# Retention and a GELU layer on one core: turned rows 8 bytes apart, v on SyncE's queue, and a shorter warm-up

## The chip, the cores and the metric

The kernel runs on one core of a Trainium2 chip. The core has TensorE (PE) for matrix products, VectorE (DVE), ScalarE (ACT) and GpSimd (POOL) for elementwise work, and SyncE (SP), which here only starts transfers. Transfers can be started from the queues of SP, ACT and POOL. The metric is device time in microseconds (us), the median of several runs.

## The reference

Eight batches of eight heads; 576 tokens, 64 values a head. Each score is weighted with a decay that depends on the distance of the two tokens, and nothing after the query counts. The heads of a token, side by side, are the 512 inputs of a two-layer network with exact GELU.

```python
scores = scale * np.matmul(q, k.transpose(0, 1, 3, 2))
gamma = 1.0 - 2.0 ** (-5.0 - np.arange(H, dtype=np.float32))
rel = pos[:, None] - pos[None, :]
Dmat = np.where(rel >= 0, gamma[:, None, None] ** rel[None, :, :], 0.0)
ret = np.matmul(scores * Dmat[None], v)
x = np.ascontiguousarray(ret.transpose(0, 2, 1, 3)).reshape(B * S, H * D)   # 4608 x 512
h = x @ w_in                                                                # 512 x 2048
out = (0.5 * h * (1.0 + erf(h / sqrt(2)))) @ w_out                          # 2048 x 512
```

All inputs and the output are fp32; the kernel computes in bf16 with fp32 sums.

## The kernel before

**Chunks and units.** A sequence of 576 tokens is cut into four chunks of 128 and a tail of 64. A unit is one chunk of one batch, 128 tokens with all eight heads; the tails of two batches make one unit. There are 36 units and nine blocks of four units (512 tokens) for the network. Groups (up to two units, the same chunk of the two batches of a pair) go through the retention together: 22 groups, of which the first four are single first chunks.

**Retention of a group.** Within a chunk the decay is split: a key's part is multiplied into v (`scaled_v`, giving `vh`, with the factors `dv`), a query's part is multiplied into the result (`evacuate`, factors `dqT`), and a mask of zeros and ones stands between (`masked`, factors `msk`). Earlier chunks come in as a state u = sum of k v, kept by `state` and applied by `cross`. For a first chunk (`raw`: units 0 to 3, 18, 19, 27, 28) there is no state; its mask `near` holds the whole decay, its v goes into `inner` unscaled, and its result is only cast, by DVE or ACT, whichever the planner finds earlier free (`either`).

**Turning q and k.** Scores need q and k with the head values on the partitions. Up to group 7, PE turns them (`turn`) and DVE or ACT copies the result. From group 8 on (`BY_DVE`) they are loaded in another shape: partition p of a 32-row block holds tokens 4p to 4p+3 (tails: 2p and 2p+1), and `turn_dve` transposes blocks of 32 by 32 elements of 4 bytes, each a pair of bf16 values, on DVE. The turned rows of one token then stand side by side with those of the other tokens of its partition, so that neighbours in DVE's writing order are 16 bytes apart (8 in a tail). `scores` and `cross` read them with `cols, y`: every second bf16 value, 128 columns in a row. `state` needs k unturned too, so from unit 11 on (groups of two units) k is loaded a second time (`kn`).

**Loads.** POOL's queue starts the loads, which convert to bf16 on the way, in the order of the list `ORDER` and then group by group as `reload` adds them: q, k, second k, v. At most eight are on their way: each issue waits for the one eight earlier. Only unit 0's q and k come as fp32, over the queues of SP and ACT, and are cast. SP's queue starts the output stores. POOL also scales v for units 26 and up.

**The network.** Each block is two layers of products, `hT` then `oT`; most are done with seven half-size products in place of eight (`mlp2_fast` with accumulators `fa`, `fb`; for the last three blocks `mlp1_fast` with `ha`, `hb`), for which DVE forms sums of operands (`g_sum`, line 675, and others). They start as soon as four units have their x.

**Who sets the order.** Nothing is decided on the chip. While the program is built, a planner keeps an estimated clock for each engine (`T`, advanced by `on` and `pe`), picks the retention step or product that it estimates to be ready, and writes the instructions of every engine in that order. An engine then works strictly in its order and waits for semaphores. Before the first data come, PE runs products of zeros (`warm`, and eight at line 1050). Constants such as `dv`, `dqT` and a first small Gelu that loads ACT's table (`warm_act`) wait in the list `later` until the planner's clock has reached their time.

Of the kernel before, what the change touches and what calls it, by code (L numbers as in the profile page):

```python
# [9 lines left out]
FP32 = mybir.dt.float32  # L10
# [7 lines left out]
def kernel(  # L18
# [46 lines left out]
    raw = [i for i in range(N_U) if units[i][1] == 0]  # L65
# [4 lines left out]
    N_LD = 5  # L70
    N_QKT = 3
    N_KN = 4
    VH_POOL = 26
# [8 lines left out]
    FPOOL = 0.55  # L82
# [28 lines left out]
    zeros = const.tile([128, 512], BF16, name="zeros")  # L111
# [10 lines left out]
    nc.scalar.activation(step, lgT, AF.Exp, scale=float(C))  # L122
    val = const.tile([128, 1, 128], FP32, name="val")
    pos = const.tile([128, 1, NCI], FP32, name="pos")
    far = const.tile([128, 1, 128], FP32, name="far")
    ident = const.tile([128, 1, 128], BF16, name="ident")
    near = const.tile([128, 2, HP, 128], FP32, name="near")
    msk = const.tile([128, 1, 128], FP32, name="msk")
    msk2 = const.tile([128, 1, TAIL], FP32, name="msk2")
# [3 lines left out]
    dqT = const.tile([128, HP, S - C], FP32, name="dqT")  # L133
# [36 lines left out]

    def make_dq(hp):
        nc.scalar.activation(dqT[:, hp, 0:C], val[:, 0, :], AF.Exp, scale=lgT[:, hp], bias=off[:, hp])
# [3 lines left out]
    later += [(9.0, "act", 0.41, lambda hp=hp: make_dq(hp)) for hp in range(HP)]  # L176
    later += [(9.0, "act", 1.45, lambda: nc.scalar.activation(warm_act, ln_scale, AF.Gelu))]
# [32 lines left out]
    def tiles_of(i):  # L210
        g = groups[group_of[i]]
        if i not in loaded:
# [3 lines left out]
            else:  # L216
# [9 lines left out]
                loaded[i] = (qk, ld_pool.tile([128, H, D], BF16, tag="v", bufs=9, name="v_ld"), kn)  # L226
        return loaded[i]

    def load(what, i):
# [8 lines left out]
        if what == "dq":  # L238
            assert i - 1 in dq_done
            dq_done.add(i)  # L240
            finish_later()
            n = min(C, S - i * C)
            nc.gpsimd.tensor_tensor(dqT[:, :, (i - 1) * C:(i - 1) * C + n], dqT[:, :, (i - 2) * C:(i - 2) * C + n],
                                    step.to_broadcast([128, HP, n]), op=ALU.mult)
            on("pool", 1.2)
            return
# [19 lines left out]
        src = {"q": q, "k": k, "n": k, "v": v}[what]  # L266
        for jj in (j,) if j is not None else range(2):
            n = C if j is not None else TAIL
            if what == "n":
                dst = kn[:, :, jj]  # L270
            elif what == "v":
# [4 lines left out]
            land[what, i] = sw_dma(0.9, 0.9) if j is not None else sw_dma(0.68, 0.5)  # L276

    tiles_of(0)
    land["q", 0], land["k", 0] = 4.5, 4.6
    cast_due = {("q", 0): (loaded[0][0][:, 0], first["q32"]), ("k", 0): (loaded[0][0][:, 1], first["k32"])}  # L280
    ORDER = ("wi0 io k1 q1 v0 v1 wi1 q2 k2 v2 wi2 k3 q3 v3 wi3 wi4 wi5 wi6 wi7 wo0 wo1 wo2 wo3 wo4 wo5 wo6 wo7 "
# [894 lines left out]
```

## Time and profile before

| | |
|---|---|
| median of 3 runs (lowest, highest) | 300.25 us (299.87, 300.6) |
| the profiled execution, and its span | 299.83 us, 298.1 us |
| granted TensorE clock, mean | 0.996 |
| busy in the span: PE, DVE, ACT, POOL | 285.2 us, 231.2 us, 135.9 us, 158.2 us |
| PE products and weight loads in the profile | 3693 and 3720 |
| bytes read and written by transfers | 42.47 MB, 9.44 MB |

The page cuts the span into 40 equal slices of 7.45 us and gives each engine a digit, its busy share in tenths. A group of instructions is one line of the kernel with one operation: number, busy time in us, mean duration in ns, then the idle time of the engine ahead of them and what ended it. A row of the waits names who waited, for whom, the total in us, how often and the longest. A row of the timeline gives start, length, engine, line, operation, output and inputs. Products overlap: a product's record goes on past the start of the next.

### The profile page before, as it was taken

To read this page: it belongs to the slowest core of one execution; us is meant where nothing else is said; L and a number is where in the kernel's file an instruction comes from. 1 tells how busy PE (TensorE), PEld (TensorE's weight loads), DVE (VectorE), ACT (ScalarE), POOL (GpSimd) and SP (SyncE) were. 2 spreads that over 40 slices of the span, in tenths; PEclk is the share of its full clock that TensorE was granted. 3 is DMA by queue.
4 is the path that set the end of the run, shared out by engine and by line. 5 is a ranking of instruction groups with operands and counts; after the bars stand their busy time and mean duration, and the time that the engine had idled before them with its cause. 6 is when DMAs were issued, how large, how long until landed. Compare 5 with 4: busy or idle time off the path is not lost.

```text
span 298.1 us, 8709 instructions
## 1 busy us (share of the span) xinstructions
PE 285.2 (96%) x3693; PEld 211.5 (71%) x3720; DVE 231.2 (78%) x430; ACT 135.9 (46%) x262; POOL 158.2 (53%) x231
## 2 busy tenths in 40 slices
PE   7999999998999999999999999999999999999994
PEld 2578656887756656766666656567888888888883
DVE  3872039999999999996770699847997999898851
ACT  5546315844254354343445433534453555546421
POOL 8976798899999988989889941000000000000000
PEclk9999999999999999999999999999999999999998
DMA  9999999999999999999999610201001201201114
GB/s 141 168 186 204 182 170 189 166 135 131 121 162 135 138 141 150 110 160 120 192 151 132 78 38 2 73 2 37 35 2 70 74 0 73 71 2 62 45 55 124
DMA packets 111415, 31.50 MB, mean 106 GB/s; under 512 B 89105, under 2 KB 107025, under 8 KB 111377
## 3 DMA queue, kind: packets, MB, share of 16 engines
q0 software_dynamic: 103744, 20.99, 83.8%
q1 hardware_dynamic: 6592, 9.70, 9.6%
q8 instruction: 29, 0.48, 0.6%
q10 hardware_dynamic: 1040, 0.26, 0.4%
q14 instruction: 10, 0.07, 0.1%
HBM read 42.47 MB, written 9.44 MB: 174 GB/s over the span
## 4 chain that ended last, share of the span: by engine, by line
PE 46%; POOL 24%; DMA 13%; DVE 9%; issue 5%; ACT 1%; DVEq 0%; POOLq 0%; ACTq 0%
PE fa L707 13%; POOL qkb_ld L261 11%; PE fb L707 10%; PE hT L603 7%; PE ha L812 7%; DMA qk_ld<-in_q_dram 6%; PE hb L812 5%; POOL v_ld L275 5%; DMA qkb_ld<-in_q_dram 3%; DMA w_out<-in_moe_w_out_dram 3%; POOL early L275 3%; DVE ret L452 2%; POOL w_in L234 2%; DVE qkT L380 2%; DVE s L675 1%
## 5 line engine op out<-in xcount | busy, mean ns | idle before, releaser
L603 PE MATMUL hT<-x,w_in 128*128 128x512 bf16 (+2 forms) x522 | 92.2, 314 | 2.0 <-DVE x L333 0.5
L603 PEld LDWEIGHTS <-w_in 128*128 128x128 bf16 x544 | 49.4, 98 | 24.5 <-issue 0.9
L707 PEld LDWEIGHTS <-g_all 128*128 128x128 bf16 x512 | 49.5, 98 | 11.6 <-issue 0.7
L608 ACT ACTIVATE g_all<-hT 128x512 bf16<-128x512 f32 x64 | 38.1, 597 | 42.6 <-PE hT L603 40.0
L707 PEld LDWEIGHTS <-s 128*128 128x128 bf16 x384 | 37.0, 98 | 8.3 <-issue 0.3
L693 DVE TENSOR_TENSOR o_sb<-fb,t 128x256 f32<-128x256 f32 x48 | 19.9, 416 | 22.3 <-ACT t L335 11.7
L817 ACT ACTIVATE g_all<-tt 128x512 bf16<-128x512 f32 x36 | 22.6, 630 | 30.2 <-DVE tt L825 30.1
L261 POOL DMA_DIRECT2D qkb_ld<-in_k_dram x56 | 31.1, 594 | 5.6 <-DMA v_ld<-in_v_dram 2.6
L707 PE MATMUL fa<-w_out,g_all 128*128 128x256 bf16 x256 | 33.1, 273 | 0.1
L452 DVE TENSOR_TENSOR ret<-sc,msk 128x512 bf16<-128x512 f32 x48 | 29.6, 671 | 2.8 <-PE sc L425 1.7
L261 POOL DMA_DIRECT2D qkb_ld<-in_q_dram x56 | 31.1, 593 | 0.3 <-issue 0.3
L275 POOL DMA_DIRECT2D v_ld<-in_v_dram x36 | 30.4, 862 | 1.4 <-DMA w_out<-in_moe_w_out_dram 0.8
L825 DVE TENSOR_TENSOR tt<-hb,tt 128x512 f32<-128x512 f32 x36 | 24.5, 687 | 5.2 <-ACT tt L335 2.8
L611 ACT ACTIVATE g_all<-hT 128x512 bf16<-128x512 f32 (+1 forms) x36 | 19.4, 549 | 14.4 <-PE hT L603 14.2
L380 DVE STREAM_TRANSPOSE qkT<-qkb_ld 128x512 f32<-128x512 f32 (+1 forms) x28 | 25.0, 945 | 0.0
L335 ACT COPY t<-fa 128x256 f32<-128x256 f32 x35 | 13.0, 371 | 21.1 <-PE fa L707 21.1
L275 POOL DMA_DIRECT2D kn_ld<-in_k_dram x22 | 19.8, 907 | 2.0 <-DMA qkb_ld<-in_q_dram 1.1
L812 PEld LDWEIGHTS <-ws 128*128 128x128 bf16 x192 | 18.8, 98 | 2.2
L583 DVE TENSOR_TENSOR x<-o_ps,dqT 128x512 bf16<-128x512 f32 (+1 forms) x32 | 18.2, 608 | 1.2 <-PE o_ps L560 1.2
L333 DVE COPY qkT<-qk_ps 128x512 bf16<-128x512 bf16 x10 | 3.9, 419 | 17.4 <-PE qk_ps L368 17.4
L707 PE MATMUL fa<-wt,g_all 128*128 128x256 bf16 x128 | 16.5, 273 | 0.2 <-ACT t L335 0.2
L707 PE MATMUL fb<-w_out,s 128*128 128x256 bf16 x128 | 16.4, 273 | 0.2
(112 smaller groups left out, 455.3 us busy)
## 6 DMA issues: line engine op xcount, KB each, us to landing
out_dram<-o_sb SPq DMA_DIRECT2D x31, 256.0 KB, 2.7
v_ld<-in_v_dram POOLq DMA_DIRECT2D x28, 128.0 KB, 4.7
qkb_ld<-in_q_dram POOLq DMA_DIRECT2D x44, 64.0 KB, 4.2
qkb_ld<-in_k_dram POOLq DMA_DIRECT2D x44, 64.0 KB, 3.7
kn_ld<-in_k_dram POOLq DMA_DIRECT2D x22, 128.0 KB, 4.3
w_in<-in_moe_w_in_dram POOLq DMA_DIRECT2D x8, 256.0 KB, 6.9
w_out<-in_moe_w_out_dram POOLq DMA_DIRECT2D x8, 256.0 KB, 10.0
out_dram<-o_sb SPq DMA_DIRECT2D x8, 128.0 KB, 3.0
```

The lines of the kernel that those rows point to most:

```text
L261: nc.gpsimd.dma_start(qk[p0:p0 + 32, "qk".index(what), 0:HP * per].rearrange("p (h x) -> p h x", h=HP), {"q": q, "k": k}[what][2 * bp + jj ...
L275: nc.gpsimd.dma_start(dst, src[2 * bp + jj, :, ci * C:ci * C + n, :].rearrange("h s d -> s h d"))
L380: nc.vector.transpose(dst, src)
L452: nc.vector.tensor_tensor(r, t, by, op=ALU.mult)
L603: nc.tensor.matmul(hT[:, m - m0, :], lhsT=w_in[:, cc, m * 128:m * 128 + 128], rhs=x_tiles[t][:, cc, lo:hi], start=(cc == 0), stop=(cc == N ...
L608: nc.scalar.activation(g_all[:, t % 2, :, m0, :], hT.rearrange("p n (a c) -> p (n a) c", a=2), AF.Gelu)
L611: nc.scalar.activation(g_of(t, 2 * lo // TOK)[:, m0:m0 + n, lo_:lo_ + hi - lo], hT, AF.Gelu)
L693: nc.vector.tensor_tensor(dst, src, f[key], op=ALU.add)
L707: nc.tensor.matmul(dst, lhsT=x[:, kk, :], rhs=y[:, kk, :], start=(name in "125" and kk == 0), stop=(kk == HK - 1), skip_group_check=True)
L812: nc.tensor.matmul(dst[:, m, :], lhsT=a[:, cc, c0:c0 + 128], rhs=y[:, cc, :], start=(name in "125" and m == 0 and cc == 0), stop=(cc == HC ...
L817: nc.scalar.activation(g_of(t, part)[:, m0:m0 + 2], src, AF.Gelu)
L825: nc.vector.tensor_tensor(f[key], f["b"][1], f[key], op=ALU.add)
```

## The change

- The turned rows of a long group are written in two halves of two tokens a partition each, so that neighbours are 8 bytes apart. For queries the halves are tokens 4p, 4p+1 and 4p+2, 4p+3, and `turned_q` reads them back in the natural order; for keys the halves are the even and the odd tokens, and `turned_k` reads them one after the other.
- Everything that stands with a key follows its order: the second k (`kn`) and v are loaded as two transfers of 64 rows, even tokens to partitions 0 to 63 and odd ones to 64 to 127; there is a mask `mskp` and there are factors `dvp` for that order (`make_skewed`, six small DVE operations and one on ACT).
- v of units 11 to 35 comes over SP's queue as fp32 (`load_v`, tiles `v32`, four buffers), asked for up to four units ahead of the scores; `scaled_v` reads it.
- First chunks 18, 19, 27, 28 are treated like the others: scaled v, mask, and `evacuate` with factors `dqT` for chunk 0, which POOL makes from chunk 1's by the factor `back`.
- POOL scales v from unit 20 on instead of 26. Load buffers for q and k: 4 instead of 5; buffers of turned tiles: 4 instead of 3. Some tiles share buffers (`zeros`, `far` with v32; `near` with q and k; the first turned tiles with `kn`).
- Six warm-up products instead of eight, other planner estimates, and unit 0's v is loaded ahead of unit 1's q and k.
- `put` may send the second half of a last store over ACT's queue.

```diff
-    raw = [i for i in range(N_U) if units[i][1] == 0]
+    raw = [i for i in range(N_U) if units[i][1] == 0 and group_of[i] not in BY_DVE]
-    N_LD = 5
-    N_QKT = 3
+    N_LD = 4
+    N_QKT = 4
-    VH_POOL = 26
+    VH_POOL = 20
-    FPOOL = 0.55
+    FPOOL = 0.6
+    N_V32 = 4
+    N_WARM = 6
+    V_LEAD = 4
...
+    def make_skewed():
+        p = pos[:, :, 0:1]
+        nc.vector.tensor_scalar(skew, p, 64.0, -127.0, op0=ALU.is_ge, op1=ALU.mult)
+        nc.vector.tensor_tensor(skew, skew, p, op=ALU.add)
+        nc.vector.tensor_tensor(mskp, val, skew.to_broadcast([128, 1, 128]), op=ALU.subtract)
+        nc.vector.tensor_scalar(mskp, mskp, 0.0, None, op0=ALU.is_ge)
+        nc.vector.tensor_tensor(posp, pos, skew.to_broadcast([128, 1, NCI]), op=ALU.add)
+        nc.vector.tensor_tensor(dvp, lgh.to_broadcast([128, H, NCI]), posp.to_broadcast([128, H, NCI]), op=ALU.mult)
...
+    later += [(8.5, "dve", 0.8, make_skewed), (9.0, "act", 0.3, lambda: nc.scalar.activation(dvp, dvp, AF.Exp, scale=-1.0, bias=ln_scale))]
...
+    def load_v(i):
+        bp, ci, j = units[i]
+        v32[i] = ld_pool.tile([128, H, D], FP32, tag="v32", bufs=N_V32, name="v32")
+        for e in range(2):
+            src = v[2 * bp + j, :, ci * C + e:ci * C + C:2, :] if j is not None else v[2 * bp + e, :, ci * C:ci * C + TAIL, :]
+            nc.sync.dma_start(v32[i][64 * e:64 * e + 64], src.rearrange("h s d -> s h d"))
...
+        if what == "n":
+            for e in range(2):
+                nc.gpsimd.dma_start(kn[64 * e:64 * e + 64, :, j], k[2 * bp + j, :, ci * C + e:ci * C + C:2, :].rearrange("h s d -> s h d"))
+                land[what, i] = sw_dma(0.68, 0.45)
+            return
...
-    ORDER = ("wi0 io k1 q1 v0 v1 wi1 q2 k2 v2 wi2 k3 q3 v3 wi3 ...
-             ... q11 k11 q12 k12 n11 n12 v11 v12").split()
+    ORDER = ("wi0 io v0 k1 q1 v1 wi1 q2 k2 v2 wi2 k3 q3 v3 wi3 ...
+             ... q11 k11 q12 k12 n11 n12 dq0").split()
...
+    def turned(n, x):
+        us = 1 if units[groups[n][0]][2] is None else 2
+        t = qkT_of(n)[:, x].rearrange("p h s -> p (h s)")[:, 0:HP * us * 128]
+        return us, t.rearrange("p (h u b t y) -> p h u b t y", h=HP, u=us, t=2, y=2)
...
-        dst = qkT[:, x, :, 0:rows, :].rearrange("p h s y -> p h (s y)").bitcast(FP32).rearrange("p h (b t) -> p h t b", b=32)
+        dst = qkT_of(n)[:, x].rearrange("p h s -> p (h s)")[:, 0:2 * m].bitcast(FP32)
+        if us == 1 or x == 0:
+            src, dst = src.rearrange("p h (u t) e -> p (h u) t e", u=us), dst.rearrange("p (h b t) -> p h t b", t=2, b=32)
+        else:
+            src, dst = src.rearrange("p h (t u) e -> p h t u e", u=us), dst.rearrange("p (h u b t) -> p h t u b", h=HP, t=2, b=32)
         nc.vector.transpose(dst, src)
...
+    def turned_q(n, sl, hp, y):
+        return turned(n, 0)[1][sl, hp, :, :, :, y].rearrange("p u b t -> p b u t")
+
+    def turned_k(n, sl, hp, y):
+        return turned(n, 1)[1][sl, hp, :, :, :, y].rearrange("p u b t -> p (u b t)")
...
-                            nc.tensor.matmul(dst, lhsT=qkT[sl, 1, hp, cols, y], rhs=qkT[sl, 0, hp, cols, y],
+                            nc.tensor.matmul(dst, lhsT=turned_k(n, sl, hp, y), rhs=turned_q(n, sl, hp, y),
...
-                by = near[:, e] if i in raw else msk.to_broadcast([128, HP, 128])
+                by = near[:, e] if i in raw else (mskp if group_of[i] in BY_DVE else msk).to_broadcast([128, HP, 128])
...
-        (nc.gpsimd if on_pool else nc.vector).tensor_tensor(vh, loaded[i][1], dv[:, :, ci:ci + 1].to_broadcast([128, H, D]), op=ALU.mult)
+        (nc.gpsimd if on_pool else nc.vector).tensor_tensor(vh, v32.get(i, loaded[i][1]), (dvp if i in v32 and units[i][2] is not None else dv)[:, :, ci:ci + 1].to_broadcast([128, H, D]), op=ALU.mult)
...
-                            a, b_ = u[sl, 2 * hp + y, :], qT[sl, 0, hp, cols, y]
+                            a, b_ = u[sl, 2 * hp + y, :], turned_q(n, sl, hp, y)
...
+        while v_due and v_due[0] < nV + N_V32 and v_due[0] <= nA + V_LEAD and ("q", v_due[0]) in land:
+            load_v(v_due.pop(0))
...
-            nc.sync.dma_start(out[row:row + n, lo:hi], o_sb[p0:p0 + n, lo:hi])
+            queue = nc.scalar if t == N_BLK - 1 and m and not left(runs2, t) else nc.sync
+            queue.dma_start(out[row:row + n, lo:hi], o_sb[p0:p0 + n, lo:hi])
...
-    for _ in range(8):
+    for _ in range(N_WARM):
```

## The prediction

> **What bounds the kernel now.** I read the slices, then stretches of the span cut where they change, then what TensorE (PE) waited for, then the groups with their shapes. First the slices: four rows of the page, forty slices of 7.5 us.
>
> ```profile
> PE   7999999998999999999999999999999999999994
> DVE  3872039999999999996770699847997999898851
> POOL 8976798899999988989889941000000000000000
> DMA  9999999999999999999999610201001201201114
> ```
>
> PE is full but for the first slice and the last. VectorE (DVE) is full from about 50 to 130 us, GpSimd (POOL), which issues the loads, until 165. The stretches (length; busy time and count of PE, weight loads, DVE, ACT, POOL; granted clock; DMA; GB/s):
>
> ```profile
> 20.00:55.00 35.00, 33.94 (x385) 24.01 (x390) 15.64 (x28) 16.17 (x33) 27.83 (x36) 1.00 1.94 188
> 55.00:130.00 75.00, 72.14 (x1307) 51.35 (x1313) 74.31 (x124) 34.03 (x64) 69.95 (x111) 1.00 1.43 138
> 130.00:160.00 30.00, 29.79 (x327) 19.99 (x329) 19.16 (x33) 13.35 (x26) 26.93 (x41) 1.00 1.50 154
> 160.00:210.00 50.00, 48.38 (x770) 32.77 (x778) 37.01 (x68) 20.05 (x40) 15.43 (x20) 1.00 0.31 48
> 210.00:280.00 70.00, 69.77 (x638) 62.21 (x637) 63.00 (x118) 38.09 (x68) 0.00 (x0) 1.00 0.11 39
> ```
>
> PE has the same work after the change, so the time can only move by PE's idle time, by matmul time itself, by the start and by the end. Between 20 and 210 us PE is idle for 1.06 + 2.86 + 0.21 + 1.62 = 5.75 us. The longest of its waits there:
>
> ```profile
> PE sc L407 <- DVE qkT L380: 2.0, 3, 1.2
> PE sc L407 <- DVE ret L452: 0.6, 2, 0.4
> PE hT L603 <- DVE x L333: 0.5, 1, 0.5
> PE hT L603 <- DVE x L583: 0.4, 2, 0.2
> ```
>
> All four end with DVE: 3.5 us in 8 waits. A matmul's record runs some 0.16 us beyond the start of the next (219 ns long, 56 ns apart), and this tail hides the beginning of each wait: 3.5 + 8 x 0.16 = 4.8 us of PE are lost to a late DVE.
>
> **DVE: the step of the turned rows.** The groups with shapes:
>
> ```profile
> L380 DVE STREAM_TRANSPOSE qkT<-qkb_ld 128x512 f32<-128x512 f32 x22 | 22.7, 1089 | 0.0
> L380 DVE STREAM_TRANSPOSE qkT<-qkb_ld 128x256 f32<-128x256 f32 x6 | 2.4, 418 | 0.0
> L275 POOL DMA_DIRECT2D kn_ld<-in_k_dram x22 | 19.8, 907 | 2.0 <-DMA qkb_ld<-in_q_dram 1.1 <-issue 0.7
> L463 POOL TENSOR_TENSOR vh<-v_ld,dv 128x512 bf16<-128x512 bf16 x10 | 10.8, 1133 | 5.1 <-PE u_ps L504 4.0 <-issue 1.1
> ```
>
> The short tile (2 tokens a partition) writes its 4-byte elements 8 bytes apart, the long one (4 tokens) 16 apart. Doubling 256 elements at one per DVE cycle of the short one's slope would give about 418 + 267 = 685 ns; the long one takes 1089. The changed kernel writes all 8 apart: 22 x (1089 - 685) = 8.9 us less DVE. VectorE also loses the scaling of v (vh) for units 20 to 25, 6 x 0.675 (L463 on DVE) = 4.05 us, and gains the scaling of four first chunks (units 18, 19, 27, 28), which are plain casts on ACT now: 4 x 0.674 = 2.7 us. Scaling from fp32 instead of bf16 I price at nothing: ret and vh, 512 elements from fp32 and from bf16, take 671 and 675 ns. Net -10.2 us on DVE between 70 and 185 us, where it is busy over 80%. Of PE's 4.8 us I take three quarters, -3.6; ends 0 (something else late at the same places) and -7 (all idle time with its hidden parts).
>
> **POOL and SP.** Off POOL go the v loads of units 11 to 35: 22 x 0.89 us and 6 of 64 rows x 0.75 = 24.1. The second copy of k goes from 22 issues of 128 rows to 44 of 64; the 64-row v issues took 0.68 to 0.82, so 44 x 0.70 - 20.0 = +10.8. Six scalings more are 6 x 1.10 = +6.6, one dqT more +1.07 (L243). Net -5.6 us of POOL up to 165 us, in front of the q and k loads: transfers per pair of units on that queue stay 12. SP takes 50 issues at about 0.45 (its 128-row q load): 22 us in a queue that mostly waits. New waits: (a) the v loads stand behind output stores, which wait for DVE; (b) 16 scalings on POOL wait for SP's v, and behind the first seven stand the q and k loads that the transposes and then PE's scores need; (c) with four load buffers instead of five, group 8's q load waits for group 4's state product, done near 47 us while POOL gets there at 52.4, so nothing. The cover for (a) and (b): v is asked for up to four units ahead of scores, about two groups of 8 us. (d) While POOL scales, L675 sums on DVE took 0.83, 0.94 and 1.29 us instead of 0.68, 1.0 us in all with 10 scalings; 16, earlier, may add 0.6. For (a) to (d) I take +1.0 us on PE, one wait of the longest kind now (1.2); ends 0 and +3.
>
> **Order on PE.** The built programs' order shows 133 changes between kinds of PE work before and 122 after. Eight products that follow another kind take longer in the chain, 0.99 against 0.87:
>
> ```profile
> 112.10 0.87 PE fa L707 x8
> ...
> 113.89 0.58 PE o_ps L560 x31
> 114.47 0.99 PE fb L707 x8
> ```
>
> 11 x 0.11 = -1.2 us; ends 0 and -1.5.
>
> **The start.** ACT's rows:
>
> ```profile
> 11.03 0.58 ACT L335 CAST x<-o_ps 128x512 bf16<-128x512 f32 x1 [5.41 <-PE o_ps L489]
> 11.51 0.33 ACT L175 ACTIVATE dv<-pe_arg,ln_scale 128x40 f32<-128x40 f32 x1
> 11.74 1.64 ACT L172 ACTIVATE dqT<-val,off,lgT 128x128 f32<-128x128 f32 x4
> 13.39 1.28 ACT L177 ACT_TABLE_LOAD   x1
> 14.69 0.20 ACT L177 ACTIVATE warm_act<-ln_scale 128x1 f32<-128x1 f32 x1
> ```
>
> Now the first chunk's x comes first. In the changed program it stands last, behind dv, dqT, the new dvp, the table load and warm_act, and dvp waits for six more small DVE operations. Step by step: the first transposes no longer stand behind nine warm products (6.71 us); the casts let them go near 5.6, and the first masks end near 9.15 instead of 10.30. DVE's constants then take 1.44 (11.03 to 12.47 now) and about 1.1 for the new six (the two 128x128 of far 0.23 and 0.29, four of 0.15): 11.7. dvp 0.33, load 1.28, warm_act 0.20: 13.5; x 0.58: 14.1 against 11.61. The first MLP products start at 14.15 instead of 12.87; the second chunk's scores stand behind them on PE and their copies behind x on ACT, 2 x 0.6: 15.2 instead of 11.24. Followed on to the fourth chunk, PE has about 1.8 us less useful work behind it. Half comes back: the 1.06 us of idle between 20 and 55 is PE out of MLP work while loads are due, and the work left over fills it. I take +0.9; ends -0.7 (only the shorter warm-up counts) and +2.3. The earlier v of chunk 0 gains nothing where x waits.
>
> **The end.** The program's order shows the last stores all still on SP; no store is on ACT's queue. This part does not do what it says: 0, no range.
>
> **Sum:** +0.9 - 3.6 - 1.2 + 1.0 = -2.9 us. The profiled execution took 299.83 (span 298.1), so 296.9 in its terms; the median is 0.42 above it: 297.3.
>
> **Rivals.**
> *Queries read in hops (slower).* Keys stay 4 bytes apart, but the queries that PE streams now come two at a time, 4 bytes apart, then two from 256 bytes further on, and back. No row shows such a stream; the nearest are today's scores (L407), 4 bytes apart in one run, 32 products in 0.57 to 0.64. If PE reads them at half rate, each set of 32 long products takes 8 x 53 ns = 0.43 us more, in 11 score and 9 state-to-output sets: 20 x 0.43 = 8.6 us, all on PE: 297.3 + 8.6 = 305.9. It decides from 2.9 / 20 = 0.15 us a set. For it: the transposes show that steps can cost. Against: they lost at one element in each 16 bytes, and the short one, two in 16, was at full rate. Chance 0.12.
> [...]
> *The start costs in full and queues bite.* Start +2.3, new waits +2.5, DVE gain halved to -1.8, order -1.2: +1.8, 302; from 299.7 up. For it: the fixed order cannot react to a late v. Chance 0.17, of which 0.07 lies within 0.6 us of no change.
> *More gain.* Start -0.7, DVE -5, order -1.2, waits +0.5: -6.4, 293.8. For it: the longest PE waits after 20 us all end with DVE. Against: the ACT order above. Chance 0.14.
> *As summed:* 295 to 299.6, chance 0.57.
>
> **Range and chances.** Leaving out half-rate reads and the far ends: 293.5 to 301.5. Two timings of this kernel differ by up to 0.2%, 0.6 us: faster 0.14 + 0.57 = 0.71, same 0.07, slower 0.10 + 0.12 = 0.22.
>
> **What would show it.** Long transposes near 0.69 us; DVE under 9 in some slices between 50 and 130; PE's wait for qkT near 0; first MLP products at about 14.1 us; 32-product score sets still at 0.57 to 0.64; 64-row kn issues near 0.7. The prediction is wrong if those sets grow, if PE waits for vh or v, or if PE's idle time between 20 and 210 stays near 5.75.

## The result, and the profile after

The changed kernel takes 303.3 us (median of 20 runs, 301.94 to 307.4) against 300.38 us for the kernel before (299.67 to 300.95): a ratio of 1.0107 with a 95% interval of 1.008 to 1.0134. It is slower by about 1%. Runs over 1.5% above the fastest of their kernel are in no ratio here (three of these 20, two of experiment 8, five of 9, and one of 13 that took 414.6 us at a clock of 0.66 and is in no range either); medians are of all runs. The forecast was 297.3 us, 293.5 to 301.5, with 0.71 for faster.

The changed kernel's runs lie in two clumps: 13 from 301.9 to 304.1 us with a mean granted clock of 0.997 to 1.0, and seven from 306.0 to 307.4 with 0.986 to 0.994. The profiled one took 306.2 us (span 304.1), so it is read together with a second profile of the same kernel (304.59 us, experiment 16), and the causes are taken from experiments where they can be.

Three rows of the page of the changed kernel, forty slices of 7.6 us:

```profile
PE   7699999879999999999999999999999999999994
DVE  4572019999998989713995959864998999899761
PEclk9979999999999999999999999999999999999999
```

DVE did get room, though not much: between 50 and 137 us slices with 8, 8 and 7 stand where it had nines, then 1 and 3 where it had 6 and 7. But PE loses more in the second slice, and in the third the clock is down. Stretches of the same trace, with the columns as before the change:

```profile
20.00:55.00 35.00, 33.62 (x388) 23.29 (x386) 14.88 (x26) 16.59 (x33) 28.30 (x37) 1.00 1.97 184
55.00:130.00 75.00, 72.42 (x1147) 52.09 (x1147) 69.26 (x119) 32.65 (x62) 66.19 (x112) 1.00 1.30 159
130.00:160.00 30.00, 29.50 (x394) 20.19 (x393) 18.90 (x31) 13.26 (x26) 21.61 (x34) 1.00 0.86 119
160.00:210.00 50.00, 49.57 (x827) 32.86 (x828) 35.02 (x66) 18.86 (x36) 18.75 (x25) 1.00 0.53 95
```

DVE is busy 69.3 of 75 us in place of 74.3, and from 55 to 210 us it has 123.2 us of work in place of 130.5: 7.3 us less, not the 10.2 of the sum. PE's idle time from 20 to 210 us is 1.38 + 2.58 + 0.50 + 0.43 = 4.89 us in place of 5.75. That is 0.9 us less, where I had counted on some 2.6 (3.6 less the 1.0 of new waits), and the span is 6.0 us longer all the same. So the loss lies in PE's own work and ahead of 20 us. One of the signs of being wrong stands in the list of PE's waits, which had no such row before:

```profile
PE o_ps L539 <- DVE vh L513: 1.3, 2, 1.1
```

The groups with their shapes, first two of the kernel before, then those of the changed one:

```profile
L407 PE MATMUL sc<-qkT 32*128 32x128 bf16 x352 | 7.7, 215 | 2.7 <-DVE qkT L380 2.0 <-DVE ret L452 0.6
L560 PE MATMUL o_ps<-qkT,u_sb 32*64 32x128 bf16 x288 | 5.9, 217 | 0.3 <-ACT u_sb L521 0.3
```

```profile
L425 DVE STREAM_TRANSPOSE qkT<-qkb_ld 128x512 f32<-128x512 f32 x22 | 14.7, 694 | 0.0
L457 PE MATMUL sc<-qkT 32*128 32x128 bf16 x352 | 9.5, 248 | 0.5 <-issue 0.3 <-DVE qkT L425 0.2
L610 PE MATMUL o_ps<-qkT,u_sb 32*64 32x128 bf16 x288 | 7.6, 248 | 0.0
L300 POOL DMA_DIRECT2D kn_ld<-in_k_dram x44 | 30.3, 718 | 12.3 <-PE u_ps L554 9.2 <-DMA qkb_ld<-in_q_dram 1.5 <-issue 1.2
```

The long transposes fell from 1089 to 694 ns (685 was worked out), and the 64-row issues of the second k take 0.72 us (0.70). The long products of scores and of state-to-output, however, take 248 ns each; they took 215 and 217. From the first product of a set of 32 to the first product behind it, 0.77 to 0.78 us pass where 0.57 to 0.58 did: 0.20 us a set, and there are 20 sets.

At the start, ACT's rows of the profiled execution (start, length, engine, line):

```profile
9.50 1.63 ACT L191 ACTIVATE dqT<-val,off,lgT 128x128 f32<-128x128 f32 x4
11.72 0.33 ACT L196 ACTIVATE dvp<-dvp,ln_scale 128x40 f32<-128x40 f32 x1 [0.58 <-DVE dvp L188]
12.05 1.28 ACT L197 ACT_TABLE_LOAD   x1
13.34 0.20 ACT L197 ACTIVATE warm_act<-ln_scale 128x1 f32<-128x1 f32 x1
13.45 0.57 ACT L370 CAST x<-o_ps 128x512 bf16<-128x512 f32 x1
```

The first x stands last, at 13.45 us (13.5 was worked out), and PE's first MLP products start at 14.07 us (14.15), the second chunk's scores at 15.05 (15.2), as the prediction followed them. What it did not see is what PE does meanwhile, and the stretch behind it:

```profile
14.07 0.61 PE L653 MATMUL hT<-x,w_in 128*128 128x128 bf16 x8 [2.54 <-ACT x L370]
```

```profile
14.80:18.30 3.50, 3.25 (x22) 1.68 (x24) 1.89 (x3) 1.65 (x4) 3.50 (x6) 0.51 1.99 174
```

PE stood for 2.54 us, and right after that the granted clock (the third column from the right) is 0.51 for 3.5 us.

### The profile page after: what moved, and what is told of

Its sections match the earlier page's. It is cut to its first block, busy times and chain, and to the rows that moved or that the text cites. A ratio compares the mean times of both kernels' runs of the same rounds, so it can differ in the third digit from the quotient of the medians.

```text
span 304.1 us, 8823 instructions
## 1 busy us (share of the span) xinstructions
PE 290.4 (95%) x3720; PEld 215.1 (71%) x3720; DVE 226.4 (74%) x430; ACT 136.7 (45%) x264; POOL 153.2 (50%) x232
## 4 chain that ended last, share of the span: by engine, by line
PE 78%; DVE 16%; issue 3%; ACT 2%; DVEq 0%
PE hT L653 20%; PE fa L757 17%; PE fb L757 13%; PE ha L862 7%; PE hb L862 5%; DVE ret L502 3%; PE oT L686 3%; PE sc L457 3%; PE o_ps L610 3%; DVE s L725 2%; PE o_ps L539 2%; DVE x L633 2%; DVE vh L513 2%; DVE qkT L425 1%; PE warm L1104 1%
## 5 line engine op out<-in xcount | busy, mean ns | idle before, releaser
L653 PE MATMUL hT<-x,w_in 128*128 128x512 bf16 (+2 forms) x544 | 93.4, 317 | 4.1 <-ACT x L370 2.5
L743 DVE TENSOR_TENSOR o_sb<-fb,t 128x256 f32<-128x256 f32 x48 | 20.1, 420 | 24.3 <-PE fb L757 13.6
L300 POOL DMA_DIRECT2D kn_ld<-in_k_dram x44 | 30.3, 718 | 12.3 <-PE u_ps L554 9.2
L502 DVE TENSOR_TENSOR ret<-sc,mskp 128x512 bf16<-128x512 f32 x44 | 27.1, 679 | 2.0 <-PE sc L457 2.0
L633 DVE TENSOR_TENSOR x<-o_ps,dqT 128x512 bf16<-128x512 f32 (+1 forms) x36 | 20.9, 623 | 0.8 <-PE o_ps L610 0.6
L513 POOL TENSOR_TENSOR vh<-v,dvp 128x512 bf16<-128x512 f32 x14 | 15.0, 1119 | 6.0 <-DMA v<-in_v_dram 5.9
L425 DVE STREAM_TRANSPOSE qkT<-qkb_ld 128x512 f32<-128x512 f32 (+1 forms) x28 | 17.1, 637 | 0.0
L757 PE MATMUL fb<-w_out,g_all 128*128 128x256 bf16 x128 | 16.6, 273 | 0.0
L757 PE MATMUL fa<-wt,s 128*128 128x256 bf16 x128 | 16.4, 273 | 0.0
```

The lines of the kernel that those rows point to most:

```text
L300: nc.gpsimd.dma_start(kn[64 * e:64 * e + 64, :, j], k[2 * bp + j, :, ci * C + e:ci * C + C:2, :].rearrange("h s d -> s h d"))
L425: nc.vector.transpose(dst, src)
L502: nc.vector.tensor_tensor(r, t, by, op=ALU.mult)
L513: (nc.gpsimd if on_pool else nc.vector).tensor_tensor(vh, v32.get(i, loaded[i][1]), (dvp if i in v32 and units[i][2] is not None else dv)[ ...
L633: nc.vector.tensor_tensor(x[:, :, n * y:n * y + n], o, dqT[:, :, ci * C:ci * C + n], op=ALU.mult)
L653: nc.tensor.matmul(hT[:, m - m0, :], lhsT=w_in[:, cc, m * 128:m * 128 + 128], rhs=x_tiles[t][:, cc, lo:hi], start=(cc == 0), stop=(cc == N ...
```

## The experiments

Each kernel was timed beside the kernel before. Theory A: the hops in which PE reads the queries are the loss. Rival B: the late start is.

**Hops moved to the other side of the product.** The queries are read in one run as they lie, and the columns are put in natural order where the product writes them to PSUM.

```diff
-        return turned(n, 0)[1][sl, hp, :, :, :, y].rearrange("p u b t -> p b u t")
+        return turned(n, 0)[1][sl, hp, :, :, :, y].rearrange("p u b t -> p (u b t)")
...
+    def natural(o):
+        return o.rearrange("p (b u t) -> p u b t", u=2, t=2)
```

> The changed kernel, but the queries are read in the order in which they lie (128 columns 4 bytes apart in one run), and the hop is made where the product writes its columns to PSUM: two columns side by side, then two from four columns on. All else, the order of the instructions too, stays. Theory A (reading the queries in hops costs PE 0.20 us in each of the 20 long sets): sets of 32 long products go from 0.77 back to 0.57 us, and the time falls by 20 x 0.20 = 4.0 us, from 303.3 to about 299.3. A2 (any hop in a product's columns costs, on the PSUM side as much as on the reading side): sets stay at 0.77, time 303.3. Rival B (the late start is what made the changed kernel slower, the sets are hidden): time 303.3, within 0.5, whatever the sets do.

Its groups:

```profile
L460 PE MATMUL sc<-qkT 32*128 32x128 bf16 x352 | 7.2, 215 | 1.7 <-issue 1.5 <-DVE qkT L425 0.2
L615 PE MATMUL o_ps<-qkT,u_sb 32*64 32x128 bf16 x288 | 5.8, 217 | 0.0
```

The sets are back at 0.57 us, so the reading costs and the writing does not. The time: median 302.67 us, in two clumps again. Five runs at full clock lie at 299.5 to 300.9 (median 300.15, against 302.43 for the changed kernel's 13 such runs: -2.3 us), seven with a mean clock of 0.989 to 0.994 at 302.5 to 303.7. Neither theory had a second loss that comes and goes. The profiled run (302.85 us) is one of the seven: PE waits 1.0 us for the first x and keeps full clock there, but it stops twice in the midst of a set, for 1.5 and 2.0 us, and behind the second stop the clock is at half, from 144.5 us on. So the upper clump of this kernel need not come from the start.

**Queries 16 bytes apart again.** Only the query tiles go back to the old layout.

```diff
+        if us == 2 and x == 0:
+            dst = dst.rearrange("p (h b t) -> p h t b", h=HP, t=4)
```

> The changed kernel, but the long query tiles are written as before the change, neighbours 16 bytes apart and in natural order, so that the products read them in one run; the keys keep their halves. The planner's estimates are untouched, so the order stays. Theory A: sets back to 0.57 us, -4.0 us; the 11 long query transposes go back to 1.09 us, 11 x 0.40 = 4.4 us more of DVE, of which between nothing and a half reaches PE: 299.3 to 301.5. Rival B (start): 303.3 to 305.5, since only DVE work is added. If 8 bytes matter to the transposes only by where the queries land, the 11 long key transposes stay at 0.69.

302.12 us (300.8 to 302.8). Products 216 and 226 ns, so the sets are short again; long transposes 901 ns in the mean of both kinds. The 4.0 us did not show. The slow query transposes are back too, and by experiments 1 and 6 the short sets give some 2.3 us and these transposes cost some 2.0, so little was to be gained: the five runs with a clock of 0.996 or more have a median of 302.03, 0.4 us under the changed kernel's at full clock. The profiled execution (302.63 us, clock 0.993) shows a further loss. PE's rows of its timeline:

```profile
139.56 0.29 PE L558 MATMUL u_ps<-vh,kn_ld 128*32 128x64 bf16 x13
142.69 0.36 PE L558 MATMUL u_ps<-vh,kn_ld 128*32 128x64 bf16 x19 [2.83 <-issue]
```

PE stops after 13 of 32 products that all read the same tiles, for 2.83 us, and no engine or transfer is named as the one that ended it. The clock in the 3.5 us behind is 0.51 again. More on this wait below (experiment 16).

**Unit 0's v later.** The start of before, by one string.

```diff
-    ORDER = ("wi0 io v0 k1 q1 v1 wi1 ...
+    ORDER = ("wi0 io k1 q1 v0 v1 wi1 ...
```

> The changed kernel, but unit 0's v is loaded after unit 1's k and q again, as before the change. In the program's order ACT then casts the first chunk's x ahead of dv, dqT, dvp and the table load. Rival B (the start is what cost): x on ACT near 10.3 us instead of 13.45, first MLP products near 12.9 instead of 14.07, PE's wait of 2.54 us for x gone, no low granted clock in the slice after it, and the time falls by 1.2 to 4 us, to between 299.3 and 302. Theory A alone (the hops are all that cost, the start is made up later by work left over): the start moves as said, but the time stays within 0.6 us of 303.3; sets stay at 0.77 us.

301.76 us, 301.3 to 301.8: one narrow clump at full clock. x is cast at 11.04 us and the first MLP products start at 12.89 us, as in the kernel before. So the late x costs 303.3 - 301.76 = 1.5 us in the median, and 302.43 - 301.76 = 0.7 us among the runs at full clock. The program's order tells why it was late: with v there sooner the planner scaled it before the first result was cast, and `scaled_v` calls `finish_later`, which puts all that is still waiting in `later` (dqT, dvp, the table load) on ACT ahead of x. The edit for a sooner v made x later.

**Hops alone, in the kernel before.**

```diff
-rhs=qkT[sl, 0, hp, cols, y],
+rhs=hops(qkT[sl, 0, hp, cols, y], short),
...
+        return a if short else a.rearrange("p (u b t) -> p b u t", u=2, t=2)
```

> The kernel before, with one edit: the 128 columns of queries of a long set are read in the hop order of the changed kernel (two 4 bytes apart, two from 256 bytes further on, and back). The columns of a chunk then come out in another order, so the output of units from group 8 on is permuted and is not the reference's; the amount of work is the same. Theory A: the long sets go from 0.57 to 0.77 us, and the time rises by 20 x 0.20 = 4.0 us, to 304.4. If something else of the changed kernel lengthens its sets (the tiles' place, the keys' order, the fp32 v): sets stay at 0.57 and the time at 300.4.

```profile
L410 PE MATMUL sc<-qkT 32*128 32x128 bf16 x352 | 9.8, 247 | 2.2 <-DVE qkT L380 1.7 <-DVE ret L455 0.3
L563 PE MATMUL o_ps<-qkT,u_sb 32*64 32x128 bf16 x288 | 7.6, 248 | 0.1
```

The same 0.77 us a set, from the reading order alone. The time rises to 302.47 us (ratio 1.0078, interval 1.0066 to 1.009): 2.15 us, not 4.0. The other half seems to be taken up by waits that PE has anyway: its idle time from 20 to 210 us falls from 5.75 to 3.0 us, since a set that ends 0.2 us later finds a late DVE less late.

**Both mended.** PSUM hops and v later.

> Both mendings in one: the changed kernel with the hop on the PSUM side and with unit 0's v loaded after unit 1's k and q. If the two losses add (hops in the sets; late x at the start, with the half clock that follows a long wait of PE), the sets take 0.57, PE is at full clock in the first 20 us, and the time is 301.76 less 2 to 4 us, 297.8 to 299.8, under the kernel before. If the time given back by shorter sets is taken again by another wait (PE out of its code, the second key, v), it stays above 300.4, and that wait stands in the list of PE's waits between 95 and 150 us.

Six runs at full clock: 298.4 to 299.6, median 298.98, so 2.8 us under the kernel with v later alone. Six more with a mean clock near 0.994: 300.2 to 302.6. All together 299.89 us, ratio 0.9993 (0.9965 to 1.0021): no difference from the kernel before can be told. The start is mended here, and half the runs still show a lower clock; the profiled run is not one of them, so where they lose it stays open. PE's longest waits from 20 to 210 us in a profile of 299.07 us:

```profile
PE u_ps L557 <- issue: 0.9, 1, 0.9
PE fb L762 <- DVE o_sb L748: 0.8, 1, 0.8
PE o_ps L532 <- DVE vh L516: 0.7, 1, 0.7
```

None of the three is among the waits of the kernel before. The last two stand behind v's scaling: `vh` itself, and sums on DVE that take 1.18 to 1.54 us beside POOL's scalings. The first is a stop in the midst of a set.

**One part alone, the transposes of the queries.** The kernel before, with the 11 long query tiles written 8 bytes apart and the hop at PSUM.

```diff
+        if rows == C and x == 0:
+            src, dst = src.rearrange("p h (u t) e -> p (h u) t e", u=2), dst.rearrange("p h (u b t) -> p (h u) t b", u=2, b=32)
```

> The kernel before, with one part of the change alone: the 11 long query tiles are written 8 bytes apart; the products read them in one run and place the columns in PSUM. Keys, v, loads, masks, the start and the order of all instructions stay. My step (three quarters of what DVE gives back where PE waits for it reaches PE): 11 x 0.395 = 4.3 us less DVE, 4.3 / 10.2 of 3.6 = 1.5 us less, 298.9; PE's waits for qkT (2.0 us in the kernel before) shrink to about 1. Rival (DVE was not what held PE; another engine is late at the same places): within 0.6 us of 300.4.

298.33 us (298.05 to 298.58), ratio 0.993, interval 0.9919 to 0.9941. 4.4 us less DVE, 2.0 us less time, and PE's wait for qkT goes from 2.0 to 1.0 us. The step on DVE's relief was right, and this small part beats both kernels.

**The start's wait filled.** Ten more products of zeros where PE waits for x.

```diff
-        for _ in range(n):
+        for _ in range(n + (10 if 10.1 < T["pe"] < 10.5 else 0)):
```

> The changed kernel, with ten more products of zeros in PE's wait for the first x (11.5 to 14 us). Nothing else moves; x stays late. If the half clock after that wait is what puts the changed kernel's runs near 306 us in place of 302 to 303, there is no low clock between 10 and 20 us, and all runs lie near 302.3. If the clumps have another cause (PE's code coming late, transfers), the runs still lie in two clumps. If the late x itself is the loss: 302.3 stays 0.5 above the kernel with v later (301.8).

303.11 us, 301.8 to 304.4. Its clock from 14.8 to 18.3 us is 1.00, its six runs have clocks of 0.997 or more, and none of them lies near 306. This fits the half clock after the wait as what makes the upper clump, but does not settle it: where seven in 20 lie high, none in six would come by chance about one time in 13, and the profile of experiment 1 and the runs of experiment 5 have lower clocks that this wait does not explain. Nor can a half clock of 3.41 us cost more than 1.7 us, where the clumps lie 3.7 apart. Filling the wait does not take away the lower clump's loss.

**Only dv made early.** v stays first, but scaling it pulls only `dv` forward.

```diff
-        if len(later) > HP + 3:
-            finish_later()
+        while any(x[3] is make_dv for x in later):
+            _, engine, dur, fn = later.pop(0)
+            fn()
+            on(engine, dur)
```

> The changed kernel with the hop on the PSUM side; v of unit 0 stays first, but its scaling pulls only dv's own making ahead of the first x on ACT, not all that is left over (dqT, dvp, table load). x should come near 10.4 us. If v sooner is worth something once ACT's order is right, the time is under that of the kernel with v later and PSUM hops, by up to 1 us (297 to 299.5); if not, equal to it within 0.6.

300.11 us, but from 296.9 to 302.7. The two best runs (296.9 and 297.0) are under the forecast of 297.3, ten are above it. Among the runs at full clock the median is 299.92, 0.9 above experiment 5, so a sooner v has gained nothing. The profiled run (302.7) has two stops of PE in the midst of a set (1.4 and 1.5 us) and a sum on DVE of 4.02 us.

**v over SP's queue alone.** The kernel of experiment 6, with v of 21 units as fp32 over SP. The load buffers for q and k go from 5 to 4, as in the change.

```diff
+            nc.sync.dma_start(v32[i][64 * e:64 * e + 64], src.rearrange("h s d -> s h d"))
...
-tensor_tensor(vh, loaded[i][1], dv[
+tensor_tensor(vh, v32.get(i, loaded[i][1]), dv[
```

> The kernel before with the queries 8 apart (298.3 us), and one more part of the change: v of 21 units comes as fp32 over SP's queue, two transfers of 64 rows each, three buffers, instead of over POOL's queue; load buffers for q and k 4 instead of 5, as in the change. Keys, first chunks, start and the engines that scale v stay. Theory C (v's transfers on SP's queue delay the 16-KB blocks of PE's own program, so that PE runs out of code in the dense stretches of small products): waits in the midst of sets that end 1.3 to 1.6 us after such a block has landed appear between 95 and 150 us, 1 to 4 us in all, and the runs scatter over 2 us or more, 298.5 to 302. Rival D (the blocks are late because the changed kernel's order packs more small products together, not because of transfers): no such waits, runs within 0.6 us of each other, at 298.3 or under, since POOL has 21 issues of 0.89 us less.

302.96 us, 298.9 to 305.0 (ratio 1.0015, 0.9985 to 1.0045), where experiment 6 stays within 0.6 us. So v over SP, with the buffers that go with it, brings the scatter. It has only one stop in the midst of a set (0.6 us at 121 us), which the trace puts down to DVE. The long wait is another one. DVE's row, POOL's and PE's, each from its own timeline of the profiled run (303.29 us):

```profile
154.70 4.11 DVE L699 TENSOR_TENSOR s<-g_all,s 128x1024 bf16<-128x1024 bf16 x1
```

```profile
154.15 1.07 POOL L485 TENSOR_TENSOR vh<-v_ld,dv 128x512 bf16<-128x512 bf16 x1
155.16 3.08 POOL L485 TENSOR_TENSOR vh<-v,dv 128x512 bf16<-128x512 f32 x3
```

```profile
160.70 1.60 PE L731 MATMUL fb<-w_out,s 128*128 128x256 bf16 x8 [2.66 <-DVE o_sb L717]
```

A sum that takes 0.68 us alone lasts 4.11 us beside four scalings of v in a row on POOL, and ends 0.6 us after the last of them. PE waits 2.66 us for the work that stands behind it on DVE, and runs its next 3.4 us at a clock of 0.50.

**v back on POOL's queue.** From experiment 8, with v of the groups turned by DVE loaded by POOL, in two transfers of 64 rows, and twelve buffers for them.

```diff
+                nc.gpsimd.dma_start(v_ld[64 * e:64 * e + 64], v[2 * bp + j, :, ci * C + e:ci * C + C:2, :].rearrange("h s d -> s h d"))
```

> The changed kernel with PSUM hops and with only dv made early (300.1 median, 296.9 to 302.7), but v of the groups turned by DVE comes as bf16 over POOL's queue again, two transfers of 64 rows each; nothing but stores and the first q is left on SP's queue. POOL gets 44 issues of about 0.70 us and six of 0.75 more. Theory C: PE's waits in the midst of sets go (0.3 us or less in all, from 3.3), and the runs lie within 1.5 us of each other; the time is 297 to 300 if POOL's longer queue (35 us more) costs PE nothing to 3 us. Rival D: waits in the midst of sets stay 1 to 4 us and the scatter over 3 us stays.

305.93 us, 305.7 to 306.7 in four runs. The scatter is gone, and no sum takes longer than 0.92 us. PE's longest waits now end with work that ACT and DVE do late. I put this down to POOL, which no run shows by itself:

```profile
130.00:160.00 30.00, 30.00 (x302) 20.01 (x300) 14.33 (x26) 13.86 (x27) 30.00 (x49) 1.00 1.23 125
160.00:210.00 50.00, 46.31 (x884) 31.59 (x882) 34.34 (x63) 17.35 (x34) 39.70 (x57) 1.00 0.81 90
```

POOL (fifth pair) is full until 200 us, and the loads come later. The key order makes v cost two issues of 0.7 us (the second k's issues of 64 rows took 0.72) in place of one of 0.9 (0.89 in the kernel before), so with this key order POOL's queue has no room for v. One stop in the midst of a set stays, 0.6 us at 204.5 us.

**Experiment 6 with the mended start of the change.** Six warm products, v first, only dv early, and the change's estimates for the start.

> The kernel before with the queries 8 apart (298.3) and the change's start as it could have been: six warm products, unit 0's v first, and only dv made ahead of the first x on ACT. No SP transfers of v, no hops on reading. The first x comes on ACT near 10.4 us instead of 11.03 and the first MLP products near 11 to 12 instead of 12.87. If that start is worth something: 0.5 to 1.5 us less, 296.8 to 297.8. If the work behind only fills other idle time later: 298.3 within 0.3. If the order that the planner finds from there is worse: above 298.6.

298.55 us, ten of twelve runs from 297.95 to 298.92. The first MLP products start at 11.93 us in place of 12.87 in the kernel before (13.6 in the profile of experiment 6), and the time stays: a start that is 0.9 us sooner is worth nothing here. In the profile (299.92 us, one of the other two runs) PE's idle time from 20 to 55 us is 2.4 us where experiment 6 has 0.7, so what came sooner is waited for again. A wait of 1.1 us at 51.2 us is followed by a half clock of 3.41 us there.

**Every v scaled on DVE**, from experiments 8, 9 and 3, and from 6 as the control.

```diff
-    VH_POOL = 20
+    VH_POOL = 99
```

> The changed kernel with PSUM hops and only dv made early (e8: 300.1 median, 296.9 to 302.7), and every v scaled on DVE instead of the last 16 units on POOL. DVE gets about 14 x 0.68 = 9.5 us of work, where it is busy 66 of 75 us and 20 of 30. Theory i (POOL's scalings hold DVE's sums, and PE then waits): every sum of 1024 takes 0.69, PE's wait for o_sb near 155 us goes (0.8 to 1.6 us), the runs lie closer together and at 297 to 299. Theory ii (late program blocks): waits in the midst of sets stay at 1 to 3 us and the runs still scatter by 3 us or more, 297 to 303. Rival: DVE's 9.5 us cost more than the held sums did, all runs above 300.

> The kernel before with the queries 8 apart and v over SP's queue (e9: 302.96 median, 298.9 to 305.0), and every v scaled on DVE instead of the last 10 units on POOL. Theory i: no sum of 1024 beyond 0.75, PE's wait of 2.66 us for o_sb near 158 us and the half clock after it go; runs at 298 to 300, within 1.5 us of each other. Theory ii: as before, waits in the midst of sets and a scatter of over 3 us. If a late v itself now holds DVE (DVE waits for v's transfer ahead of its other work), PE waits for DVE by another name and the time stays above 300.

> The changed kernel with unit 0's v later (e3: 301.76, 301.3 to 301.8), and every v scaled on DVE. The hops stay, so the sets take 0.77. Theory i: PE's wait of 1.51 us for o_sb and the sum of 3.98 us go, 300.3. If DVE's 9.5 us more cost as much: 301.8 within 0.5. If they cost more: above 302.3.

> The kernel before with the queries 8 apart (e6: 298.33), v over POOL's queue as before, and every v scaled on DVE instead of the last 10 units on POOL: 10 x 0.68 = 6.8 us more DVE, most of it after 130 us. If DVE's work is what made e13 slower than e6, this lies near e13, 300 to 301. If v over SP's queue is, it lies within 0.6 us of e6, 297.7 to 298.9.

In all four every sum of 1024 is at 0.68 to 0.69 us. The group that held the long sum, of experiment 9 and then of 13:

```profile
L699 DVE TENSOR_TENSOR s<-g_all,s 128x1024 bf16<-128x1024 bf16 x16 | 14.3, 896 | 0.0
```

```profile
L699 DVE TENSOR_TENSOR s<-g_all,s 128x1024 bf16<-128x1024 bf16 x16 | 10.9, 683 | 0.0
```

| scaled on DVE | with POOL's scalings | without |
|---|---|---|
| from 8 | 300.11 (296.9 to 302.7) | 298.9 (297.9 to 301.5) |
| from 9 | 302.96 (298.9 to 305.0) | 301.0 (300.5 to 301.7) |
| from 3 | 301.76 (301.3 to 301.8) | 301.52 (301.2 to 302.4) |
| from 6, no v over SP | 298.33 (298.1 to 298.6) | 300.21 (299.6 to 300.4) |

The wide scatter of 9 goes with POOL's scalings, so the held sums are the likely cause of it; the order of PE's work changed as well. The level of 298 to 300 that theory i gave for 13 did not come. The control shows the price: 6.8 us more work on DVE cost 1.9 us. Of the 2.7 us by which 13 lies above 6, 1.9 are that work and 0.8 are v over SP with its buffers. From 3, where no run showed a half clock, the held sums went and DVE's 9.5 us came, and the time stayed. In 12 the stops in the midst of sets are nearly gone too (one, 0.4 us by the products' starts, against two of 1.7 in 8), which I had not expected. Theory ii had forecast that they stay; the order of PE's work changed with DVE's load, so the run does not tell which of the two ended them.

**The changed kernel once more**, one run.

> The changed kernel once more, for a second profile. If it takes about 302.3: full clock after PE's wait for the first x, and the same wait of about 2.5 us; the 4 us to the profile that took 306.2 are then 1.7 us of half clock and 2 us of other waits, to be named. If it takes about 306: half clock of 3.41 us again, after a wait near 12 to 14 us.

304.59 us, which neither 302.3 nor 306 foresaw, and the clock is 1.00 from 10 to 210 us. PE waited only 1.3 us for x. In the first profile the clock had risen at 8.0 us, and PE's work ahead of that wait ended at 11.5; here it rose at 10.2 us, seven earlier products of zeros took 2.9 us in place of 2.0, and that work ended at 12.8. In place of the half clock it has two stops in the midst of sets. PE's timeline:

```profile
107.63 0.50 PE L457 MATMUL sc<-qkT 32*128 32x128 bf16 x15
109.07 0.57 PE L457 MATMUL sc<-qkT 32*128 32x128 bf16 x17 [0.94 <-issue]
```

```profile
142.35 0.29 PE L554 MATMUL u_ps<-vh,kn_ld 128*32 128x64 bf16 x13
144.24 0.33 PE L554 MATMUL u_ps<-vh,kn_ld 128*32 128x64 bf16 x19 [1.60 <-issue]
```

The queues of the core name a candidate. From 141.7 to 142.8 us:

```profile
q1 hardware_dynamic: 594, 0.15, 67.3%
q0 software_dynamic: 136, 0.06, 40.4%
q8 instruction: 1, 0.02, 5.5%
```

Queue 8 carries 29 blocks of 16 KB in every run, 0.48 MB: 64 bytes for each of PE's 7,440 products and weight loads, so I took these for PE's program. In this stretch one of them comes in beside SP's and POOL's transfers; it landed at 142.75 us, and PE went on at 144.24, 1.49 us later. The same holds for every such stop of at least 0.25 us that ends with "issue" in the profiles of the changed kernel and its variants, 17 of them, from 0.3 to 3.0 us long between two products' starts: each ends 1.3 to 1.6 us after a block of queue 8 has landed. In the kernel before and in its variants 4, 6, 9, 11, 13 and 15 there is none that ends so. In 14 of the 17, all but those of two profiles with records missing (12 and 16), the stop stands behind exactly 256 k + 193 of PE's records (products, weight loads and a few records for semaphores), where k blocks have landed, with k from 10 to 21. As 256 records of 64 bytes are 16 KB, these are boundaries between blocks. I read these stops as PE standing for the next block of its program; no run changed the program's loading by itself, so this is not shown alone.

The lengths fit as well. At these 14 stops the block lands 2.5 to 5.4 us after PE passed the boundary before, and PE has used up the 256 records in between in 3.1 to 6.0 us; where landing and the 1.3 to 1.6 us behind it take longer than PE's own work, PE waits. In experiment 2 these were 4.7 + 1.4 us against 3.1, a stop of 3.0. A dense run of small products is thus one half of it and a late block the other. What makes the block late stays open: SP's transfers of v alone do not (9, 13 and 14 have them and no such stop; 10 has none of them on SP and still one stop).

## Why the prediction was wrong

**The rival that decided: queries read in hops.** The prediction gave it 0.12 and a price of 0.43 us a set, "decides from 0.15 us a set". It measured 0.20 us in each of the 20 sets, half the price, above that point. The price's 53 ns for 128 columns at full rate is near what the products of before show (eight of 256 columns in 0.87 us: 54 ns for 128); that hops would halve the rate was an assumption. The step that failed is its being priced at nothing in the sum, with the argument that two elements in 16 bytes ran at full rate in DVE's short transpose (418 ns for 256 elements, where other DVE operations on 256 took 411 to 416). That row was of another engine, of writing, and of one direction; it did not carry over to PE's reading. Put alone into the kernel before, the reading order costs 2.15 us (experiment 4). Undone, it gives back 2.3 us (experiment 1) or 2.8 (3 against 5) among the runs at full clock; by the medians of all runs 0.6 and 1.9, since the upper clumps differ. The gross 4.0 us never shows in full.

**The start.** The three times that count in the prediction's working came out within 0.15 us (x 13.45, MLP 14.07, scores 15.05), and +0.9 was taken. Measured: 0.7 in the runs at full clock, +1.5 in the median (experiment 3). The difference is the upper clump, seven of 20 runs with clocks of 0.986 to 0.994. One half clock of 3.41 us takes 0.006 off the mean of a run, so these fit one or two of them; the one profile among them has it behind PE's wait for x, which no step had. The idle time from 20 to 55 us, which was to give half of the start back, is 1.38 us, not less than the 1.06 before.
All six half clocks inside a span took 3.41 us (the clock was 0.51 over 3.5 us in the changed kernel and in experiment 2, and 0.50 over 3.4 us in 9). The wait of PE just ahead was 1.1 us in experiment 11, 1.4 in 8, 2.0 in 1, 2.54 in the changed kernel, 2.66 in 9 and 2.83 in 2, while waits of 1.50 to 1.55 us in experiments 1, 3 and 7 were followed by full clock. So the length of the wait alone does not tell whether a half clock follows.

**DVE's relief, -3.6: the rate holds, the amount was smaller.** The 685 ns of a long transpose was an estimate: the 267 ns it adds for 256 more elements stand in no row, but DVE operations on fp32 took 411 ns for 256 elements and 671 for 512, 260 more, and the long transposes came to 694. 4.4 us less on DVE gave 2.0 us (experiment 6), 6.8 us more cost 1.9 (experiment 15): 0.46 and 0.28 of DVE's time, around the 3.6 / 10.2 = 0.35 of the sum. PE's waits for qkT fell from 2.0 to 0.2 us as forecast. But DVE got 7.3 us of room between 55 and 210 us, not 10.2, because 2.9 us of it went into the sums of the next step.

**New waits, +1.0: mis-sized, and partly of another kind.** With hops and start mended the kernel takes 298.98 us at full clock; the forecast without its start term was 296.4. So about 2.6 us more than the 1.0 are lost, if the steps on the order and on DVE hold. The waits (a) to (d) were named, but (d), DVE's sums beside POOL's scalings, was priced by single meetings in the trace of before (0.15 to 0.6 us each, 0.6 in all). When v comes late, POOL scales several units in a row and one sum can wait for all of them: 3.3 us in experiment 3, 3.4 in 9. In the profile of the changed kernel the sums lose 4.8 us in all, where before it was 1.0; 1.8 of the 4.8 lie at 58 to 62 us around a dqT product on POOL, and PE's wait of 1.1 us for vh stands right behind them. PE's stops behind the blocks of queue 8, 0.3 to 3.0 us each, were in no step. And some of these waits bring a half clock behind them.
The rows show two forms of the meeting of DVE's sums with POOL's scalings. In experiments 3, 8 and 9 one sum ends some 0.6 us after the last of POOL's scalings. In experiment 5, where the first sum starts ahead of them, four sums and four scalings take turns, the scalings at 1.21 to 1.50 us each:

```profile
148.47 1.18 DVE L730 TENSOR_TENSOR s<-g_all 128x1024 bf16<-128x1024 bf16 x1
149.68 1.43 DVE L730 TENSOR_TENSOR s<-s,g_all 128x1024 bf16<-128x1024 bf16 x1
151.03 1.54 DVE L730 TENSOR_TENSOR g_all<-g_all 128x1024 bf16<-128x1024 bf16 x1
152.50 1.54 DVE L730 TENSOR_TENSOR s<-g_all,s 128x1024 bf16<-128x1024 bf16 x1
```

The loss on DVE is much the same, 3.0 us, but PE then waited 0.8 us for o_sb, against 1.5 in experiment 3 and 2.7 in 9.

**Order on PE, -1.2:** no run takes it alone, so it stays open. **The end, 0:** the program's order has all last stores on SP, as the prediction said.

Ledger, from 297.3: hops +2.8, start +0.6 beyond the 0.9, new waits +2.6 beyond the 1.0 (with whatever the steps on the order and on DVE missed): 303.3. The last is what is left over, so the sum had to come out. The first and last are by the runs at full clock of experiment 5; by experiment 4 hops are 0.7 less, and waits then 0.7 more.

## What to carry to other kernels

When data are laid out anew to make a writer faster, price the reader's new pattern on the reader's own engine, and see whether the hop can be put where it is free: here writing PSUM in hops of two values cost nothing (0.57 us a set, as before), and 11 transposes changed in this way alone gave 2.0 us (0.993). When work is moved to a queue that lets it arrive in bunches, price the bunch and not the single meeting: four scalings in a row can hold a sum of 0.68 us for 4 us. And a time gained at the start is worth only what no later wait takes back (experiment 11: nothing), while a wait of PE of 1 to 3 us can be followed by 3.41 us at half clock, which is up to 1.7 us more.

## What was not expected of the hardware

- PE reading 128 columns as two values 4 bytes apart, then two 256 bytes away: 0.77 us for 32 products on four row groups, against 0.57 in one run. Writing PSUM in pairs of fp32 values with steps between: 0.57.
- A half clock of 3.41 us after PE waits of 1.1 to 2.8 us, in six of 18 profiles; the three waits of over 2 us all had it behind them, others of 1.5 us had not.
- Stops of PE in the midst of a set, 0.3 to 3.0 us, each ending 1.3 to 1.6 us after a 16-KB block of queue 8 has landed, and 14 of the 17 standing at a multiple of 256 of PE's records (plus 193).
- A bf16 sum on DVE of 0.68 us that lasts 4.0 to 4.1 us beside three or four scalings in a row on POOL, or four sums of 1.2 to 1.5 us that take turns with four scalings.
